# Four banks for the scores of two head pairs, and a new order of the weighted values

## The chip, the cores and the metric

The kernel runs on one core of one Trainium2 chip. The metric is the time of one execution on the device, in microseconds (us). The engines are named as the profile names them: PE is TensorE (PEld its weight loads, which overlap the matmuls), DVE is VectorE, ACT is ScalarE, POOL is GpSimd, and SP issues the transfers (DMAs). The execution that was profiled ran at a mean granted TensorE clock of 0.999 of full speed.

## What is computed

Windowed attention with eight global keys, for 4 batches, 8 heads, 768 positions and a head size of 64, and behind it a two-layer network with a gate. The inputs are float32.

```python
scores = scale * q @ k.T                       # per batch and head, 768 x 768
keep = is_global | is_local                    # keys 0..7, or the last 96 keys
scores = where(keep, scores - slope[h] * dist, -1e9)
a = exp(scores - max); a = a / (sum(a) + 1e-9)
x = (a @ v) as (3072, 512)                     # all heads side by side
h = x @ w_in                                   # 512 -> 2048
g = h * clip(h + 3, 0, 6) / 6
out = g @ w_out                                # 2048 -> 512
```

## The kernel before

The 3072 rows of x are cut into eight blocks of 384 rows (a block is one half of a batch). Per block the attention has four head pairs, and the network has 16 slices f of 128 hidden columns. A slice is worked in two layers: `first` (L166) makes 12 matmuls of 128x384 into one PSUM bank named hp; `gate` (L177) reads that bank on ACT (L183, tile g) and on DVE (L184); `high` and `rest` split g into gh (POOL, L190) and gl (DVE, L197); `second` (L200) makes 9 matmuls of 128x512 into the three banks named acc. There is one buffer for g, so a gate waits until gl of the slice before is made.

Eight PSUM banks exist: three acc, two hp (`ps_h`, taken in turn), and one each named sp, tp and xp, which the letters s, t and x of `bank` (L232) stand for.

The program has three stages. Attention of the first blocks comes first, then a mixed stage, and then the stage that the change touches, "layers" (L645 to L661): the network of block i, for i = 2 to 7, with the attention of block i+1 strewn in between. `twos` (L490) works two slices at a time: two first layers, then the two second layers of the slices before. It yields four times for each two slices, so units 0 and 1 of every four stand behind the first layers and units 2 and 3 behind the second layers. `attention` (L713) hangs the attention of block i+1 on these units; TURNS says at which unit a pair starts. Of one pair:

- `scale` (L861): POOL multiplies the queries, one instruction (L865), a turn ahead.
- `packed` (L867): PE makes the scores of the pair, 24 small matmuls with 64 rows and 32 columns of the array, one bank for each of the two heads. The trace keeps two records of each. I call such a visit to small matmuls an excursion.
- `weigh` (L900): DVE adds the distances and takes the least value (L908), six times per pair, and ACT makes the exponentials (L912), six per pair.
- `sum_up`, `normalize` (POOL, L932, six per pair), `spread` (DVE transposes into the tile `blocks`, L954, six per pair) and `send` (L956): SP issues four DMAs from `blocks` into the tile `weights`. The pool of `blocks` has one buffer, so the spread of the next pair waits until these DMAs have landed.

When all four pairs of a block are there, `weighted` (L688) multiplies weights and values in two excursions at units 25 and 26, four pairs at a time in four banks, one of them an hp bank. `put_x` (L155) reads each bank on ACT (xh) and on DVE (xl), and the result is x of the next block.

On PE, POOL and SP the program's order holds (`in_order`, L665). On DVE and ACT a scheduler sets the order, from estimates of its own.

## Time and profile before

| | |
|---|---|
| time, median of 3 runs | 647.18 us (646.72 to 648.17) |
| the profiled execution | 647.65 us, of which the span is 645.9 us |
| PE busy | 634.3 us (98%) |
| DVE busy | 354.9 us (55%) |
| ACT busy | 255.9 us (40%) |
| POOL busy | 167.4 us (26%) |
| DMA traffic | 59.78 MB, 93 GB/s on average |

A busy share is an average over the whole span. A busy PE is not the same as a PE that does useful columns: matmuls overlap in the record, so what an excursion costs is read from the starts of the matmuls around it. Times in rows count from the start of the span.

### The profile page before, as it was taken

How to read it: one execution, taken by the hardware profiler on the slowest of the kernel's cores; microseconds unless marked ns; L12 is line 12 of the kernel's file. 1: busy time of each engine (PE TensorE's matmuls, PEld its weight loads, DVE VectorE, ACT ScalarE, POOL GpSimd, SP SyncE). 2: the span in 40 equal slices, each digit the busy share in tenths (PEclk: the TensorE clock that was granted, in tenths of full speed). 3: DMA queues.
4: the chain of work that ended last, by engine and by line, in shares of the span. 5: the costliest groups of instructions: out<-in, count | busy, mean ns of one | idle time of the engine just before them, and what ended most of it. 6: DMA issues, size and time to landing. Idle time of an engine off the chain costs nothing.

```text
span 645.9 us, 14423 instructions
## 1 busy us (share of the span) xinstructions
PE 634.3 (98%) x5593; PEld 557.5 (86%) x5593; DVE 354.9 (55%) x1066; ACT 255.9 (40%) x706; POOL 167.4 (26%) x371
## 2 busy tenths in 40 slices
PE   9989999999999999999999999999999999999997
PEld 7768999888888888888888888888888888899985
DVE  5889999996645552455534564255623555222222
ACT  5897877775415321242223231143212522221111
POOL 4668000000422441124302332033311242012100
PEclk9999999999999999999999999999999999999999
DMA  7675554543334421242232241223312311110001
GB/s 280 173 227 178 161 159 135 159 135 126 96 73 144 100 79 31 71 123 70 60 98 75 63 102 48 67 79 86 92 31 69 106 33 31 33 50 1 1 1 54
DMA packets 34334, 59.78 MB, mean 93 GB/s; under 512 B 3280, under 2 KB 21200, under 8 KB 33488
## 3 DMA queue, kind: packets, MB, share of 16 engines
q1 hardware_dynamic: 33968, 58.50, 31.4%
q8 instruction: 46, 0.75, 0.5%
q14 instruction: 32, 0.26, 0.1%
q10 hardware_dynamic: 288, 0.26, 0.1%
HBM read 41.16 MB, written 6.29 MB: 73 GB/s over the span
## 4 chain that ended last, share of the span: by engine, by line
PE 89%; DVE 4%; ACT 3%; DMA 1%; POOL 1%; issue 1%; SPq 0%; POOLq 0%; ACTq 0%; DVEq 0%
PE hp L172 40%; PE acc L204 36%; PE sp L879 2%; DVE xl L159 2%; PE sp L204 2%; PE tp L204 1%; PE xp L204 1%; PE sp L706 1%; ACT n L912 1%; DMA wst<-w 1%; POOL n L932 1%; PE tp L706 1%; DMA load<-pairs 1%; PE xp L972 1%; PE sp L897 1%
## 5 line engine op out<-in xcount | busy, mean ns | idle before, releaser
L183 ACT ACTIVATE g<-hp,small 128x384 f32<-128x384 f32 x127 | 73.8, 581 | 261.3 <-PE hp L172 174.5
L172 PE MATMUL hp<-xh,w1h 128*128 128x384 f32 x512 | 174.2, 340 | 0.7 <-DVE xl L159 0.3
L172 PE MATMUL hp<-xh,w1l 128*128 128x384 f32 x512 | 172.4, 337 | 0.1
L172 PE MATMUL hp<-xl,w1h 128*128 128x384 f32 x512 | 171.7, 335 | 0.0
L190 POOL TENSOR_SCALAR gh<-g 128x384 fp32r<-128x384 f32 x104 | 53.5, 515 | 424.4 <-DVE g L184 397.6
L184 DVE SCALAR_TENSOR_TENSOR g<-g,hp 128x384 f32<-128x384 f32 x128 | 70.7, 552 | 122.0 <-ACT g L183 120.7
L204 PE MATMUL acc<-w2h,gh 128*128 128x512 f32 x336 | 133.2, 396 | 0.0
L204 PE MATMUL acc<-w2h,gl 128*128 128x512 f32 x336 | 131.9, 393 | 0.0
L204 PE MATMUL acc<-w2l,gh 128*128 128x512 f32 x336 | 131.7, 392 | 0.0
L197 DVE TENSOR_TENSOR gl<-g,gh 128x384 fp32r<-128x384 f32 x128 | 71.4, 558 | 66.4 <-POOL gh L190 59.0
L172 PEld LDWEIGHTS hp<-xh,w1h 128*128 128x128 f32 x512 | 96.1, 188 | 7.0 <-DVE xl L159 2.3
L912 ACT ACTIVATE n<-n,least 128x136 f32<-128x136 f32 (+2 forms) x192 | 79.9, 418 | 54.2 <-DVE least L908 53.4
L172 PEld LDWEIGHTS hp<-xl,w1h 128*128 128x128 f32 x512 | 96.1, 188 | 2.6
L172 PEld LDWEIGHTS hp<-xh,w1l 128*128 128x128 f32 x512 | 96.1, 188 | 0.9 <-DVE w1l L439 0.8
L932 POOL TENSOR_SCALAR n<-n,sums 128x136 f32<-128x136 f32 (+2 forms) x186 | 82.4, 460 | 39.7 <-DVE sums L923 23.8
L204 PEld LDWEIGHTS acc<-w2h,gh 128*128 128x128 f32 x336 | 63.1, 188 | 15.4 <-issue 3.8
L204 PEld LDWEIGHTS acc<-w2h,gl 128*128 128x128 f32 x336 | 63.0, 188 | 13.8 <-DVE gl L197 0.3
L204 PEld LDWEIGHTS acc<-w2l,gh 128*128 128x128 f32 x336 | 63.1, 188 | 11.3
L954 DVE STREAM_TRANSPOSE blocks<-n 128x256 f32<-128x256 f32 x138 | 51.2, 424 | 22.8 <-POOL n L932 21.4
L912 ACT ACTIVATION_READ_ACCUMULATOR n<-n,least 128x1 f32 x192 | 36.3, 189 | 0.0
L399 ACT ACTIVATE wz<-wst 128x512 f32<-128x512 f32 x32 | 21.6, 679 | 5.7 <-DVE w2l L439 3.9
L446 DVE CUSTOM_DVE_ANT_0 wz<-wz,we 128x1024 uint16<-128x1024 uint16 x32 | 22.2, 695 | 1.3 <-POOL we L404 0.9
(126 smaller groups left out, 728.6 us busy)
## 6 DMA issues: line engine op xcount, KB each, us to landing
wst<-w SPq DMA_DIRECT2D x32, 512.0 KB, 3.6
load<-pairs SPq DMA_DIRECT2D x31, 444.0 KB, 3.5
weights<-blocks SPq DMA_DIRECT2D x92, 120.0 KB, 2.4
values<-values SPq DMA_DIRECT2D x6, 1024.0 KB, 5.4
out<-o SPq DMA_DIRECT2D x23, 256.0 KB, 2.4
values<-pairs SPq DMA_DIRECT2D x9, 384.0 KB, 3.6
out<-o ACTq DMA_DIRECT2D x1, 256.0 KB, 3.0
load<-pairs SPq DMA_DIRECT2D x1, 252.0 KB
```

What stands on the lines that cost most here:

```text
L159: nc.vector.tensor_tensor(out=xl[:, pair, :], in0=ps, in1=xh[:, pair, :].bitcast(F32), op=ALU.subtract)
L172: self.nc.tensor.matmul(hp, lhsT=self.w1(w, f)[:, kt, :], rhs=a[:, kt, :], start=(n == 0), stop=(n == 3 * NKT - 1))
L183: nc.scalar.activation(out=g, in_=hp, func=AF.Relu, bias=self.three, scale=1.0)
L184: nc.vector.scalar_tensor_tensor(out=g, in0=g, scalar=6.0, in1=hp, op0=ALU.min, op1=ALU.mult)
L190: self.nc.gpsimd.tensor_scalar(out=gh, in0=g, scalar1=1.0, scalar2=0.0, op0=ALU.mult, op1=ALU.add)
L197: self.nc.vector.tensor_tensor(out=gl, in0=g, in1=gh.bitcast(F32), op=ALU.subtract)
L204: self.nc.tensor.matmul(acc[tt], lhsT=a[:, tk], rhs=self.w2(w, f), start=(f == 0 and j == 0), stop=(f == NF - 1 and j == 2))
L399: self.nc.scalar.activation(out=self.z[i].bitcast(F32), in_=words[:, :, 1].bitcast(F32), func=AF.Abs)
L446: tt(out=z, in0=z, in1=self.e.pop(i), op=ALU.add)
L912: nc.scalar.activation(out=e[:, j, lo:end], in_=e[:, j, lo:end], func=AF.Exp, bias=self.least[:, i:i + 1], scale=-1.0, accum_out=self.sums ...
L932: nc.gpsimd.tensor_scalar(out=e[:, j, lo:end], in0=e[:, j, lo:end], scalar1=over, scalar2=0.0, op0=ALU.mult, op1=ALU.add)
L954: nc.vector.transpose(out=self.blocks[:, :, t, 4 * s:4 * s + 4], in_=e[:, :, c:c + P].rearrange("p j (b q) -> p j b q", b=4))
```

## The change

Three things change, all for the stage "layers" (`weighted` is also called once at the end of the mixed stage, for three pairs).

The four pairs of a block no longer start at units 0, 5, 10 and 16, but two at unit 2 and two at unit 14. The first of the two takes an hp bank and the bank xp for its scores, the second takes sp and tp as before. DVE and ACT take the first pair head by head, so that the hp bank is read first. The second of the two pairs normalizes, spreads and sends two units later than the first. The pool `up` gets 6 buffers instead of 3. In `weighted`, pair 0, whose bank is hp, is now first in the order of the matmuls and not last.

```diff
-TURNS = (0, 5, 10, 16)
+TURNS = (2, 14)
...
-        self.up = self.pool("up", 3, side="right")
+        self.up = self.pool("up", 6, side="right")
...
-        for pair in pairs[::-1]:
+        for pair in pairs:
             bank = self.bank("xts"[pair.pr - 1]) if pair.pr else self.ps_h.tile([P, BANK], F32, name="hp")
...
-            at = units[TURNS[p]:]
-            at[0] += [me.packed] + [a.scale for a in (after,) if a] + [lambda me=me: self.load_next(me.n, False)]
+            at = units[TURNS[p // 2]:]
+            if p % 2 == 0:
+                at[0] += [lambda me=me: me.packed(True), after.scale, lambda me=me: self.load_next(me.n, False)]
+            else:
+                at[0] += [me.packed] + [a.scale for a in (after,) if a] + [lambda me=me: self.load_next(me.n, False)]
+                at = at[2:]
...
-    def packed(self):
+    def packed(self, first=False):
...
-        banks = [kk.bank(b)[:, 0:NT * PW].rearrange("p (t c) -> p t c", t=NT) for b in "st"]
+        banks = [kk.ps_h.tile([P, BANK], F32, name="hp"), kk.bank("x")] if first else [kk.bank("s"), kk.bank("t")]
+        banks = [bank[:, 0:NT * PW].rearrange("p (t c) -> p t c", t=NT) for bank in banks]
...
-        for t in range(NT):
-            self.weigh(t, [bank[:, t] for bank in banks], kk.up.tile([P, 2, PW], F32, name="n"), 0)
+        self.rows = [kk.up.tile([P, 2, PW], F32, name="n") for _ in range(NT)]
+        for heads in ((0,), (1,)) if first else ((0, 1),):
+            for t in range(NT):
+                self.weigh(t, [bank[:, t] for bank in banks], self.rows[t], 0, heads)
...
-    def weigh(self, t, sp, e, lo):
+    def weigh(self, t, sp, e, lo, heads=(0, 1)):
...
-        for j in range(2):
+        for j in heads:
```

What follows are three places of the built program, before and after.

On POOL, the attention of block 3, the first one in this stage. load_73 and load_74 are the queries of its pairs 1 and 2 (the L865 or L869 row is `scale`), gh belongs to the network, n are the normalizations. Before:

```order
L190 TENSOR_SCALAR gh<-g 128x384 x5
L865 TENSOR_SCALAR load_73<-load_73,over 128x384
L932 TENSOR_SCALAR n<-n,sums 128x136 x4
L190 TENSOR_SCALAR gh<-g 128x384 x2
L932 TENSOR_SCALAR n<-n,sums 128x136 x2
L865 TENSOR_SCALAR load_74<-load_74,over 128x384
```

After:

```order
L869 TENSOR_SCALAR load_73<-load_73,over 128x384
L869 TENSOR_SCALAR load_74<-load_74,over 128x384
L190 TENSOR_SCALAR gh<-g 128x384 x2
L939 TENSOR_SCALAR n<-n,sums 128x136 x10
L190 TENSOR_SCALAR gh<-g 128x384 x2
L939 TENSOR_SCALAR n<-n,sums 128x136 x2
```

Pair 1 is scaled at the same place as before, behind the gh of the first two slices, but its scores now follow at once on PE; the normalizations of two pairs stand together.

On ACT, the same block up to `put_x`. n,sums is the exponential of `weigh`, g the gate, xh the first half of `put_x`. Before:

```order
L912 ACTIVATE n,sums<-n,least 128x136 x6
L183 ACTIVATE g<-hp,small 128x384 x4
L912 ACTIVATE n,sums<-n,least 128x136 x6
L183 ACTIVATE g<-hp,small 128x384 x4
L158 CAST xh<-sp 128x384
L158 CAST xh<-tp 128x384
L158 CAST xh<-xp 128x384
L158 CAST xh<-hp 128x384
```

After:

```order
L920 ACTIVATE n,sums<-n,least 128x136 x12
L183 ACTIVATE g<-hp,small 128x384 x6
L158 CAST xh<-hp 128x384
L158 CAST xh<-xp 128x384
L158 CAST xh<-tp 128x384
L158 CAST xh<-sp 128x384
```

Twelve exponentials stand in one piece ahead of the next gate, and the hp bank of `weighted` is read first and not last.

On DVE, from the last sums of the block's pairs to `put_x` (blocks is the spread, L954 before and L961 after). Before:

```order
L923 RECIPROCAL sums<-sums 128x6
L954 STREAM_TRANSPOSE blocks<-n 128x2x128 x4
L184 SCALAR_TENSOR_TENSOR g<-g,hp 128x384
L197 TENSOR_TENSOR gl<-g,gh 128x384
L184 SCALAR_TENSOR_TENSOR g<-g,hp 128x384
L197 TENSOR_TENSOR gl<-g,gh 128x384
L954 STREAM_TRANSPOSE blocks<-n 128x2x128 x2
```

After:

```order
L197 TENSOR_TENSOR gl<-g,gh 128x384
L961 STREAM_TRANSPOSE blocks<-n 128x2x128 x6
L184 SCALAR_TENSOR_TENSOR g<-g,hp 128x384
L197 TENSOR_TENSOR gl<-g,gh 128x384
L184 SCALAR_TENSOR_TENSOR g<-g,hp 128x384
L961 STREAM_TRANSPOSE blocks<-n 128x2x128 x2
L197 TENSOR_TENSOR gl<-g,gh 128x384
L961 STREAM_TRANSPOSE blocks<-n 128x2x128 x4
```

The six spreads of pair 2 now stand in the same stretch as those of pair 3, ahead of them; on SP the eight DMAs of two sends follow each other with no load between.

## Rows read from the trace of the kernel before

**Rows 1.** The page, chain that ended last: shares of the span by engine.

```profile
PE 89%; DVE 4%; ACT 3%; DMA 1%; POOL 1%; issue 1%; SPq 0%; POOLq 0%; ACTq 0%; DVEq 0%
```

**Rows 2.** Timeline around one excursion: start, duration, engine, line, operation, [idle before].

```profile
205.45 0.34 PE L172 MATMUL hp<-xh,w1l 128*128 128x384 f32 x1
205.72 0.10 PEld L879 LDWEIGHTS sp<-load 64*32 64x32 f32 x1 [0.25 <-issue]
...
206.41 0.28 PE L879 MATMUL tp<-load 64*32 64x136 f32 x1
...
206.61 0.50 PE L204 MATMUL acc<-w2h,gh 128*128 128x512 f32 x1
...
206.95 0.40 PE L204 MATMUL acc<-w2l,gh 128*128 128x512 f32 x1
```

**Rows 3.** The chain in order of time: start, us, what (x24 two first layers).

```profile
295.99 4.36 PE hp L172 x24
300.35 4.12 PE acc L204 x18
304.47 4.19 PE hp L172 x24
...
326.35 2.09 PE acc L204 x9
```

**Rows 4.** Timeline behind the weighted values of block 3, PE and DVE.

```profile
260.94 0.55 DVE L159 TENSOR_TENSOR xl<-hp,xh 128x384 fp32r<-128x384 f32 x1
...
261.06 0.34 PE L172 MATMUL hp<-xh,w1l 128*128 128x384 f32 x1
261.54 0.44 PE L172 MATMUL hp<-xh,w1h 128*128 128x384 f32 x1
261.82 0.34 PE L172 MATMUL hp<-xl,w1h 128*128 128x384 f32 x1
```

**Rows 5.** Waits of PE's weight loads: us in total, times, longest.

```profile
PEld hp L172 <- DVE xl L159: 2.3, 5, 0.5
```

**Rows 6.** Timeline at the first excursion of block 3, PE and POOL.

```profile
200.46 0.30 PE L879 MATMUL sp<-load 64*32 64x136 f32 x1
...
202.39 0.52 POOL L190 TENSOR_SCALAR gh<-g 128x384 fp32r<-128x384 f32 x1 [2.04 <-DVE g L184]
202.88 0.60 POOL L865 TENSOR_SCALAR load<-load,over 128x384 f32<-128x384 f32 x1
```

**Rows 7.** Timeline of an excursion of the mixed stage that met an idle DVE.

```profile
158.16 0.73 PEld L879 LDWEIGHTS acc<-load 64*32 64x32 f32 x48 [0.37 <-POOL gh L190]
...
159.23 0.30 DVE L908 CUSTOM_DVE_ANT_0 n<-acc,dl 128x136 f32<-128x136 f32 x1 [0.61 <-PE acc L879]
...
159.57 0.41 ACT L912 ACTIVATE n<-n,least 128x136 f32<-128x136 f32 x1 [0.70 <-DVE least L908]
```

**Rows 8.** Timeline of one pair from exponentials to send (ACT, DVE, SP).

```profile
297.00 0.41 ACT L912 ACTIVATE n<-n,least 128x136 f32<-128x136 f32 x1 [4.94 <-DVE least L908]
...
299.38 0.57 ACT L183 ACTIVATE g<-hp,small 128x384 f32<-128x384 f32 x1
...
304.90 2.20 DVE L954 STREAM_TRANSPOSE blocks<-n 128x256 f32<-128x256 f32 x6 [0.56 <-POOL n L932]
...
307.13 2.54 SPq L960 DMA_DIRECT2D weights<-blocks  x4
```

**Rows 9.** Timeline of two sends close together in the mixed stage (SP and DVE).

```profile
167.59 2.69 SPq L960 DMA_DIRECT2D weights<-blocks  x4
...
172.19 0.77 DVE L954 STREAM_TRANSPOSE blocks<-n 128x256 f32<-128x256 f32 x2 [1.44 <-DMA weights<-blocks]
...
174.76 2.54 SPq L960 DMA_DIRECT2D weights<-blocks  x4
```

**Rows 10.** Last send of block 3, and the first matmul of its weighted values.

```profile
246.53 2.56 SPq L960 DMA_DIRECT2D weights<-blocks  x4
...
252.57 0.54 PE L706 MATMUL sp<-weights,values 32*64 32x384 f32 x2
```

## The prediction

> **What bounds the kernel now.** I read the shares of the chain that ended last first: PE holds 89% of it [rows 1], so time is gained where PE does less or waits less, and lost where PE comes to wait for something. Busy time cannot tell the two apart, so the second view is the timeline around one excursion [rows 2]. The reader is to look at starts. The last large matmul starts at 205.45, the second large one behind the excursion at 206.95: 1.50 us. Without an excursion the same two steps would take one first-layer pitch (4.18 / 24 = 0.17, from the 4.19 of two first layers) and one second-layer pitch (4.12 / 18 = 0.23) [rows 3]: 0.40. So an excursion costs 1.10. The starts of its 48 small records spread over 205.72 to 206.41, which is 0.69 [rows 2]; the other 0.41 goes into the turn from large to small matmuls and back. The third view is the waits of PE's weight loads: in this stage the large one is that on `put_x`, five times [rows 5], seen in the timeline behind the weighted values [rows 4]. Last I read the way of one pair through ACT, POOL, DVE and SP [rows 8, 9], because that way has to end before `weighted` starts.

> **Merged excursions.** Five blocks have four excursions each now, and two each afterwards. The 48 records of a second pair add 0.69 if they go on at the same pitch, and the turn of 0.41 is paid once and not twice. Ten turns fewer: 10 x 0.41 = **4.1 us less** [rows 2]. This is PE's own time, so nothing hides it. The bounds are 0.38 and 0.45 each, since the starts are given to 0.01 and the pitch varies by as much: 3.8 to 4.5.

> **The first layer's bank read first.** Before, the hp bank of `weighted` is the last that DVE reads (260.94, 0.55 long), and slice 15's first layer, whose bank it is, starts at 261.54, 0.48 behind the matmul before it instead of 0.17; the next matmul follows at 0.28, again 0.11 late [rows 4]. Together 0.42, five times: **2.1 us less**; without the 0.11 it is 1.6. Afterwards DVE reads this bank as the first of four, three readings of 0.55 or a little less earlier, so it is free over 1 us sooner, while 0.3 is needed. What is late next there is PE itself.

> **Pair 1 of block 3 waits for POOL.** `scale` of a pair is issued right in front of its own scores for pairs 1 and 3. In most places that is harmless: the second layers of two slices (4.12 [rows 3]) lie between the first layers and unit 2, and POOL is through by then. In block 3 there is nothing to finish yet at unit 2, so PE goes straight from the first layers into pair 0. POOL's order has the two gh first, then the scaling, which ends at 202.88 + 0.60 = 203.48 [rows 6]; the change moves none of these. Pair 0 starts at 200.46 and pair 1 could follow 0.69 later, at 201.15. PE waits 2.3, and I add 0.1 for the signal, an estimate: **2.4 us more, once** (2.3 to 2.6). Behind the waiting matmul stands all of PE's queue.

> **The weights of pair 3 come later.** This is the largest unknown. Pairs 2 and 3 start at unit 14, and `weighted` stands at unit 25. Before, the last send of block 3 starts at 246.53 and its four DMAs have landed some 4.5 later, about 251.0, while `weighted` starts at 252.57 [rows 9, 10]: 1.5 to spare. Now count from T, the start of the merged excursion. DVE's first score comes at T + 1.07 and ACT's first exponential at T + 1.41 [rows 7]. Twelve exponentials in one piece, ahead of the next gate, take twice the 2.38 that six take [rows 8]: T + 6.17. From that gate to the send of the first pair (two gates, six normalizations, six spreads) the same order stands in one place of the trace and takes 299.38 to 307.13, 7.75 [rows 8]: send of pair 2 at T + 13.9. `blocks` has one buffer, so DVE may not spread pair 3 before these four DMAs have landed. One such wait is in the trace: 167.59 to 172.19, 4.60 [rows 9]. Its four issues took 2.69; with the 2.54 of the other sends it would be 4.45. So T + 18.4 to 18.5. From there two spreads, another operation and four spreads, the order that the change has here, took 172.19 to 174.76, 2.57 [rows 9]: second send at about T + 21.0, landed at T + 25.4 to 25.7. PE meanwhile: 0.89 to the first large matmul [rows 2], 0.69 for the second pair, and then six large pieces, of which the first is 4.36 and the last 2.09, with 4.12, 4.19, 4.12 and 4.18 between [rows 3]: it stands in front of `weighted` at about T + 24.65. The wait is 0.75 to 1.05 by these rows; I take 0.95, near the upper end, since every hop adds a little that I left out. Five blocks: **4.8 us more**. For the range I allow 0.6 to 1.3 each, 3.0 to 6.5. Whoever waits here is PE with all that stands behind it; its first three pairs' weights are there and help nothing, since the fourth follows in the same queue.

> **The rest costs nothing.** Head 0's bank is wanted by the second first layer behind the excursion, at 0.89 + 0.69 and half of 4.36 behind T, T + 3.8 [rows 2, 3]. DVE reads its three scores from T + 1.07 on [rows 7], faster than ACT takes three exponentials (1.2 [rows 8]): it is free by T + 2.3. The gates come 2.4 later, behind six more exponentials [rows 8]; the banks that they free are wanted only after two first and two second layers, some 8 us on [rows 3]. If this cover failed, PE would wait at the third first layer. The buffers of `up` take away a wait of DVE that no row shows PE waiting for. `load_next` moves with the scores on SP; `scale` wants the loads only at the excursion after.

> **The sum.** -4.1 - 2.1 + 2.4 + 4.8 = **+1.0 us**. The profiled execution took 647.65, 0.47 over the median; the same step on the median of 647.18 gives **648.2**. Terms at their ends: -4.5 - 2.1 + 2.3 + 3.0 = -1.3 and -3.8 - 1.6 + 2.6 + 6.5 = +3.7, so 645.9 to 650.9.

> **Rivals.** *The weights land in time* (0.10). If POOL or DVE get through the chain a microsecond faster, the five waits vanish and the sum is -4.1 - 2.1 + 2.4 = -3.8: 643.4. For it: the spare time is only 1 us short, and the 7.75 holds pieces that depend on when gates fall. Against it: each piece is one that the trace shows in that order.

> *The merged excursion saves nothing* (0.08); this one ends slower and also means that the change doesn't do what it says. The second pair needs its own start-up: new banks and new row and column places, another 0.41. Then ten times 0.41 come back, but the five in front of `weighted` are taken out of PE's wait there: +1.0 + 4.1 - 2.1 = +3.0, 650.2. It decides if the starts of the second 48 records leave a gap of more than 0.3 behind the first. Against it: within the 48 records of one pair the array takes new weights all the time, without a gap.

> *The scores are not read out in time* (0.04). Twelve scores lie in four banks at once, read by one DVE. If DVE came 3 us late, the second first layer would wait about 1.5 us in each of ten excursions, which also lets the weights land in time: +1.0 + 15 - 4.8 = +11, 658. It would take over from a delay of 1.5 (T + 2.3 against T + 3.8). Against it: no spread and no long operation stands ahead of the scores on DVE in the new order. [...]

> The remaining 0.04 is for what I don't see.

> **How the numbers follow.** The forecast has 0.74. Its own spread, 645.9 to 650.9, holds nearly all of that, and the second rival too; 645.0 to 651.0 holds about 0.8. About 0.2% (1.3 us) is what a measurement of this kernel can tell from no change: 645.9 and 648.5 are the marks. Of the forecast's 0.74 about 0.45 lie between, 0.27 above, 0.02 below. With the first rival, and some of the unseen, faster is 0.13; with the second and third, slower is 0.42; same 0.45.

> **What would show it.** Merged excursions whose small records start over some 1.4 us with no gap inside; no wait for xl at slice 15 of blocks 3 to 7's attention; one wait of 2.4 in PE near 201 to 203.6, released by POOL; and five waits of about 0.95 at `weighted`, released by the DMAs of `weights`, with DVE's first spread of pair 3 waiting for the DMAs of pair 2 ahead of each. It would be wrong if the last waits are absent or twice as long, if `put_x` still reads the hp bank last, or if the granted clock falls in one of the new gaps.

## The result and the profile after

The changed kernel took 650.67 us (median of five runs, 648.55 to 651.5), the kernel before 647.18: a ratio of 1.005, 95% interval 1.0028 to 1.0071. It is slower by 3.5 us, half a per cent. That lies in the predicted range (645.0 to 651.0), 2.5 us above the predicted 648.2, and in the class "slower" by the prediction's own marks (above 648.5), which had 0.42 against 0.45 for "same". The execution that was profiled took 648.55, close to the forecast; the other four took 650.1 to 651.5. The profiled one ran at a mean granted clock of 1.000, the four at 0.996 to 0.997. So there are two things to explain: the sum of the edits, which the trace shows, and some 2.4 us more in the other four runs (their mean is 650.9), which it does not show.

The page of the changed kernel: busy time of each engine, the granted clock in 40 slices of the span, and the chain that ended last (PE's share is 87% now, against [rows 1]).

```profile
span 646.7 us, 14369 instructions
...
PE 631.9 (98%) x5593; PEld 558.8 (86%) x5593; DVE 352.4 (55%) x1066; ACT 254.7 (39%) x706; POOL 169.3 (26%) x371
...
PEclk9999999999999999999999999999999999999999
...
PE 87%; DVE 4%; ACT 4%; POOL 2%; DMA 2%; issue 1%; SPq 0%; POOLq 0%; DVEq 0%; ACTq 0%
```

A merged excursion in the timeline of the changed kernel (start, duration, engine, line, operation), the answer to [rows 2]: from the last large start, 228.64, to the second large one behind it, 230.85.

```profile
228.64 0.39 PE L204 MATMUL acc<-w2h,gl 128*128 128x512 f32 x1
228.96 0.30 PE L884 MATMUL hp<-load 64*32 64x136 f32 x1
...
230.57 0.44 PE L172 MATMUL hp<-xh,w1h 128*128 128x384 f32 x1
230.85 0.34 PE L172 MATMUL hp<-xl,w1h 128*128 128x384 f32 x1
```

That is 2.21 us, and nine of the ten excursions read so. The 96 small starts spread over 1.41 with no gap above 0.10. Two single excursions cost 2 x (1.50 - 0.40) = 2.20 beyond the large matmuls, the merged one 2.21 - 0.40 = 1.81: 0.39 saved, ten times 3.9.

The waits of the changed kernel (us in total, times, longest), first PE's and its weight loads', then DVE's:

```profile
PE sp L884 <- POOL load L869: 2.1, 1, 2.1
```

```profile
PEld sp L884 <- POOL load L869: 2.4, 1, 2.4
PEld hp L172 <- DVE least L916: 1.9, 9, 0.2
```

```profile
DVE blocks L961 <- DMA weights<-blocks: 20.3, 11, 2.9
```

The row of [rows 5], the first layer's wait for `xl`, has no successor. In its place stand one wait for POOL's scaling, and eleven waits of DVE for the transfers out of `blocks` (in the kernel before there was one, of 1.4). The latter come out at the weighted values. The timeline of those of block 5 shows it:

```profile
403.70 0.54 PE L706 MATMUL hp<-weights,values 32*64 32x384 f32 x2
...
404.95 0.54 PE L706 MATMUL sp<-weights,values 32*64 32x384 f32 x2 [0.37 <-issue]
...
405.30 0.78 PE L706 MATMUL sp<-weights,values 32*64 32x384 f32 x9
```

Pairs 0 to 2 start at 403.70, pair 3 (bank sp) 1.25 later. The large matmuls around it, first before and then after (the last one ahead, the second one behind):

```profile
403.28 0.40 PE L204 MATMUL acc<-w2h,gl 128*128 128x512 f32 x1
...
406.29 0.39 PE L204 MATMUL acc<-w2l,gh 128*128 128x512 f32 x1
```

```profile
403.37 0.40 PE L204 MATMUL acc<-w2h,gl 128*128 128x512 f32 x1
...
407.49 0.40 PE L204 MATMUL acc<-w2l,gh 128*128 128x512 f32 x1
```

That is 3.01 and 4.12. Measured in this way, the first halves of the weighted values (the first of their two excursions) of blocks 3 to 7 took 3.65, 3.27, 4.12, 3.26 and 4.41, against 3.01, 2.67, 3.01, 2.68 and 3.02 before: 4.3 us more together.

So the trace gives -3.9 - 2.1 + 2.4 + 4.3 = +0.7, and the span went from 645.9 to 646.7, by 0.8. That these two agree so well is in part chance, as the two executions did not run alike ahead of the stage that was changed. Here are one matmul of the mixed stage and the last matmul of all, before and after:

```profile
177.19 0.40 PE L204 MATMUL tp<-w2h,gl 128*128 128x512 f32 x1
...
640.75 0.40 PE L204 MATMUL acc<-w2h,gl 128*128 128x512 f32 x1
```

```profile
176.64 0.40 PE L204 MATMUL tp<-w2h,gl 128*128 128x512 f32 x1
...
641.25 0.39 PE L204 MATMUL acc<-w2h,gl 128*128 128x512 f32 x1
```

The profiled execution of the changed kernel was 0.55 earlier at the first of these (most of it, 0.47, was there at 27 us already), and from it to the last matmul it took 464.61 against 463.56, 1.05 more. The rows above name 0.7 of that; the other 0.35 is in no single wait. Behind the last matmul it took 0.3 more. The further 2.4 us of the other runs are the question of the experiments.

### The profile page after: what moved, and what is told of

The parts are those of the page before. It is cut to its first block, busy times and chain, and to the rows that moved or that the text cites. A ratio compares the mean times of both kernels' runs of the same rounds, so it can differ in the third digit from the quotient of the medians.

```text
span 646.7 us, 14369 instructions
## 1 busy us (share of the span) xinstructions
PE 631.9 (98%) x5593; PEld 558.8 (86%) x5593; DVE 352.4 (55%) x1066; ACT 254.7 (39%) x706; POOL 169.3 (26%) x371
## 4 chain that ended last, share of the span: by engine, by line
PE 87%; DVE 4%; ACT 4%; POOL 2%; DMA 2%; issue 1%; SPq 0%; POOLq 0%; DVEq 0%; ACTq 0%
PE hp L172 40%; PE acc L204 35%; ACT n L920 2%; PE sp L204 2%; PE tp L204 1%; PE xp L204 1%; PE hp L706 1%; PE sp L706 1%; PE hp L884 1%; POOL n L939 1%; DMA weights<-blocks 1%; DMA iv<-bounds 1%; DVE n L916 1%; PE sp L884 1%; PE tp L706 1%
## 5 line engine op out<-in xcount | busy, mean ns | idle before, releaser
L172 PE MATMUL hp<-xh,w1h 128*128 128x384 f32 x512 | 174.1, 340 | 0.0
L172 PE MATMUL hp<-xh,w1l 128*128 128x384 f32 x512 | 172.3, 337 | 0.1
L172 PE MATMUL hp<-xl,w1h 128*128 128x384 f32 x512 | 171.7, 335 | 0.0
L204 PE MATMUL acc<-w2h,gh 128*128 128x512 f32 x336 | 131.6, 392 | 0.0
L172 PEld LDWEIGHTS hp<-xh,w1h 128*128 128x128 f32 x512 | 96.1, 188 | 5.4 <-DVE least L916 1.9
L172 PEld LDWEIGHTS hp<-xl,w1h 128*128 128x128 f32 x512 | 96.1, 188 | 2.5
L172 PEld LDWEIGHTS hp<-xh,w1l 128*128 128x128 f32 x512 | 96.1, 188 | 0.9 <-DVE w1l L439 0.8
L939 POOL TENSOR_SCALAR n<-n,sums 128x136 f32<-128x136 f32 (+2 forms) x186 | 80.3, 452 | 17.1 <-DVE sums L930 12.3
L961 DVE STREAM_TRANSPOSE blocks<-n 128x256 f32<-128x256 f32 x138 | 50.6, 420 | 27.8 <-DMA weights<-blocks 20.3
```

The lines of the kernel that those rows point to most:

```text
L172: self.nc.tensor.matmul(hp, lhsT=self.w1(w, f)[:, kt, :], rhs=a[:, kt, :], start=(n == 0), stop=(n == 3 * NKT - 1))
L204: self.nc.tensor.matmul(acc[tt], lhsT=a[:, tk], rhs=self.w2(w, f), start=(f == 0 and j == 0), stop=(f == NF - 1 and j == 2))
L939: nc.gpsimd.tensor_scalar(out=e[:, j, lo:end], in0=e[:, j, lo:end], scalar1=over, scalar2=0.0, op0=ALU.mult, op1=ALU.add)
L961: nc.vector.transpose(out=self.blocks[:, :, t, 4 * s:4 * s + 4], in_=e[:, :, c:c + P].rearrange("p j (b q) -> p j b q", b=4))
```

## The experiments

Each kernel is compared with runs of the kernel before on the same chip (medians 647.31, 647.30 and 647.44 in the three groups), "against before" below. The clocks are means over the span, one for each run. The lower level behind the last matmul (0.68 over the last 1.9 us of the kernel before's profile, 0.95 over the last 2.7 us of the changed kernel's) counts in them too, so the profiled runs without a fall of the clock in the work show 0.998 to 1.000, those with one fall 0.995 to 0.997, and `e7_second_earlier`, with two, 0.993. The kernel before showed 0.998 or more in 40 of its 41 runs there.

### One part alone

`e5_values_first` is the kernel before with the second part of the change only.

```diff
-        for pair in pairs[::-1]:
+        for pair in pairs:
```

> The kernel before, with one part of the change alone: of the weighted values, the pair whose bank is the first layer's is computed and read out first (the pairs run from 0 to 3, not from 3 to 0). The prediction has 0.42 us for each of the five waits of the first layer for its left operand, so 2.1 us: a median of 645.1, and the row of that wait gone. The rival, by which the same wait only goes to the pair that is now last, which the scores behind it need: 647.2, the kernel before's time, with a wait of about 0.4 us at the start of the next bank.

Measured: 645.20 (644.94 to 645.89), 2.1 less than before, ratio 0.997, interval 0.9957 to 0.9982, clocks 0.998 to 1.000. The wait for `xl` at L172 is gone from its rows, and no gap stands in the next bank's place. The term of 2.1 holds, and this part alone makes the kernel faster.

`e6_turns_only` is the changed kernel with that line put back, so the merged excursions alone.

> The changed kernel without its second part: the weighted values are computed and read out in the order of before, pair 3 first. By the prediction's term of 0.42 us for each of five blocks the wait of the first layer for its left operand comes back: 2.1 us over the changed kernel, a median of 652.8, and the row of that wait stands again with 5 times and some 0.4 to 0.5 us. The rival: in the merged order pair 3's weights come last anyway, so starting with them makes the wait for the weights longer too, by up to one chunk's three other pairs (0.1 us), and the time is 653.3. If the two parts overlap, so that the wait for the weights already covers the other, the time stays at 650.7.

Measured: 653.90 (652.73 to 655.16), 6.6 more than before and some 3.2 more than the changed kernel. The wait for `xl` is back (PEld hp L172: 2.3, 5, 0.5), worth 2.1. That leaves about 1.1. The weighted values grew too: their first halves took 20.5 in all, 6.1 more than before, against 4.3 in the changed kernel's profile. The timeline of block 5 shows how:

```profile
406.47 0.40 PE L204 MATMUL acc<-w2h,gl 128*128 128x512 f32 x1
408.47 0.54 PE L706 MATMUL sp<-weights,values 32*64 32x384 f32 x2 [1.59 <-DMA weights<-blocks]
408.70 0.54 PE L706 MATMUL tp<-weights,values 32*64 32x384 f32 x2
```

With pair 3 first nothing runs until its weights land, 2.0 behind the last large start. With pair 3 last the other three pairs' first matmuls stand in that time, as the rows of block 5 above show. I had priced this at 0.1 at most. By these two profiles it is 0.36 each, by the 1.1 left in the medians 0.2. Its size is not settled, since the first halves vary from run to run by as much (below). The two parts of the change are thus not independent: the new order of reading also softens the wait that the merging makes.

### Where the clock falls

`e1_scale_early`: the scaling of pair 1 of block 3 is issued ahead of the block loop.

```diff
+        Pair(self, 3 * NPAIR + 1, None, False).scale()
         for i in range(2, len(self.blocks)):
...
-                at[0] += [lambda me=me: me.packed(True), after.scale, lambda me=me: self.load_next(me.n, False)]
+                at[0] += [lambda me=me: me.packed(True)] + [after.scale] * (n != 3 * NPAIR) + [lambda me=me: self.load_next(me.n, False)]
```

> The changed kernel, with one step put earlier: the scaling on POOL of pair 1 of block 3, for which TensorE waited 2.4 us between the two halves of that block's first excursion, is issued ahead of the block loop. The same values are computed. Both theories: the gap of 2.37 us in front of the second half of that excursion goes, and the excursion takes 2.2 us instead of 4.5. Theory G, by which the four runs of the changed kernel at a mean granted clock of 0.996 to 0.997 lost their further 2 to 3 us because TensorE's clock fell at this gap: every run comes back to a granted clock of 0.999 or 1.000, and the median falls by 2.3 and by 2.1 more, from 650.7 to about 646.3, 0.9 under the kernel before. Theory W, by which the clock falls at one of the five waits for the weights of pair 3 (0.6 to 1.4 us each): the clocks stay at 0.996 to 0.997 in most runs, and the median falls by 2.3 alone, to 648.4.

Measured: 648.31 (647.44 to 650.08), 1.0 more than before. The wait is gone: the excursion takes 2.35 instead of 4.5. Of eleven runs seven show 0.998 to 1.000 (647.4 to 648.5) and four 0.994 to 0.996 (649.4 to 650.1). Neither theory is right alone. With the gap of block 3 gone seven of eleven runs keep the clock, where three of ten of the changed kernel did, which points to the gap without proving it; four lose it all the same. The profiled run is one of these, and its windows (time, PE busy, granted clock, DMA) show where:

```profile
554.00:555.50 1.50, 0.00 (x0) 1.00 0.59 113
555.50:557.00 1.50, 1.50 (x80) 1.00 0.00 0
557.00:557.50 0.50, 0.50 (x41) 0.57 0.00 0
557.50:560.00 2.50, 2.50 (x34) 0.50 0.03 7
560.00:560.50 0.50, 0.50 (x2) 0.52 0.00 0
560.50:561.00 0.50, 0.50 (x4) 1.00 0.00 0
```

PE came to a gap of 2.16, from start to start, for the weights of pair 3 of block 7 (in the changed kernel's profile the costliest such wait was 1.4). After it had gone on, the clock fell to 0.50 for 3.4 us; half of that, 1.7, is the most it can have cost, an estimate from these two numbers. In this run the first halves of the weighted values took 21.1 in all, 6.7 more than before and the most of any, so part of what the earlier scaling saved was lost there.

`e4_scale_late` goes the other way:

```diff
+        for _ in range(4 if self.n == 3 * NPAIR + 1 else 0):
+            nc.gpsimd.tensor_scalar(out=q, in0=q, scalar1=1.0, scalar2=0.0, op0=ALU.mult, op1=ALU.add)
```

> The changed kernel, with four more multiplications by one on POOL ahead of the scaling of pair 1 of block 3 (0.76 us each by the two that stand there, 1.53 together, so 3.1 us); the values stay the same. Both theories: the gap in that block's first excursion grows from 2.4 to about 5.4 us. Theory G: the clock falls at this gap in every run, also the profiled one, whose windows behind the gap show a granted clock under 1.00; the median is 650.7 plus 3.1, 653.8, or some 2 us more where the longer gap costs more. Theory W: the windows behind the gap stay at 1.00, and where the clock falls it falls behind a wait of the weighted values; the median is 653.8.

Measured: 654.08 (653.63 to 654.40), 6.8 more than before; all four runs at 0.993 to 0.997. The gap is 5.1. Windows of the profiled run:

```profile
201.00:205.00 4.00, 0.00 (x0) 1.00 0.37 114
205.00:206.00 1.00, 0.40 (x20) 0.88 0.00 0
206.00:209.00 3.00, 3.00 (x48) 0.50 0.23 39
209.00:210.00 1.00, 1.00 (x7) 0.92 0.82 327
```

Again 3.4 us at the lower level, directly behind the gap. Counted from the first start behind the gap, the following large matmuls start 1.6 later than the same ones of the changed kernel's profiled run, which kept its clock: that is the price of this fall. Does the shorter gap of the changed kernel do the same? In `e6_turns_only`, where it is 2.38, the profiled run shows it:

```profile
201.00:202.00 1.00, 0.00 (x0) 1.00 0.25 28
202.00:203.00 1.00, 0.13 (x8) 0.86 0.81 259
203.00:206.00 3.00, 3.00 (x53) 0.50 0.29 83
206.00:206.50 0.50, 0.50 (x4) 0.86 0.69 206
```

Here the same count gives 1.4.

The changed kernel's own profiled run has the same gap, 2.37, and keeps the clock:

```profile
201.00:202.00 1.00, 0.00 (x0) 1.00 0.13 18
202.00:203.00 1.00, 0.03 (x5) 1.00 0.77 217
203.00:206.00 3.00, 3.00 (x60) 1.00 0.48 159
```

So the same idle time lowers the clock in some executions and not in others.

### Is it the idle time, or the wait?

`e9_filled` and `e12_late_filled` leave the wait and take away TensorE's idleness: matmuls of a constant into banks that the scores overwrite. In the first these are 144 small ones in the changed kernel; in the second, 22 of full size in the kernel with the late scaling.

```diff
+        for t in range(3 * NT if self.n == 3 * NPAIR + 1 else 0):
+            for g in range(GROUPS):
+                for j in range(2):
+                    nc.tensor.matmul(banks[j][g * GQ:(g + 1) * GQ, t % NT, 0:P], lhsT=kk.ident[j * D:(j + 1) * D, 0:GQ],
+                                     rhs=kk.ident[j * D:(j + 1) * D], start=True, stop=True, tile_position=(j * D, g * GQ))
```

```diff
+        for i in range(22 if self.n == 3 * NPAIR + 1 else 0):
+            nc.tensor.matmul(banks[i % 2][:, 0, 0:P], lhsT=kk.ident, rhs=kk.ident, start=True, stop=True)
```

> The changed kernel, with TensorE kept at work in the gap of block 3: ahead of the second half of that excursion stand 144 small matmuls of a constant into the same two banks, which the scores overwrite; at the 14.7 ns from start to start of the scores they take 2.1 us of the 2.37. The wait for POOL stays as long, and the result is the same. Theory G (TensorE's idle time is what the clock falls for): the excursion takes 4.5 us as before, but the clock no longer falls behind it; only the waits for the weights can still lower it, as in 4 of 11 runs of the kernel with the early scaling, so the median is 648.5 to 649.0 and most runs show 0.998 or more. The rival (the fall hangs on the wait for POOL or on what else runs at that place): the clocks stay at 0.996 to 0.997 in most runs and the median at 650.7. The small matmuls run late themselves and push the scores back: 0.3 to 1 us on top of either.

Measured: 648.79 (648.20 to 650.06), 1.5 more than before, nine runs of nine at 0.998 to 1.000. The small matmuls left a hole of 1.1 in their own middle, of which 0.85 is put down to issue, and so ran late: the starts of the excursion's scores spread over 4.6 instead of 3.7. Even so the median is 1.9 under the changed kernel's (2.0 when each is taken against before on its own chip, 1.3 against `after_again` in the same way). The clock of the profiled run is at 1.00 from the gap to 645 us, when the last matmul has ended.

> The kernel with the late scaling (four more multiplications by one on POOL, a gap of 5.1 us in block 3, 654.1 us with clocks of 0.993 to 0.997 in all its runs), with 22 matmuls of a constant of 128 by 128 into the two banks ahead of the second half of the excursion, which the scores overwrite; at an estimated 0.21 us each they fill 4.7 of the 5.1 us. The wait for POOL stays, and the result is the same. If the clock falls for TensorE's idle time, it stays at 1.00 behind the excursion, and the median is the changed kernel's undisturbed 648.5 plus 2.8 for the longer wait, 651.3, with up to 1 us more in runs in which it falls behind a wait for the weights. By the rival (the fall hangs on the wait itself or on the other work there) the clock falls here as it did without the filling: 654.1.

Measured: 649.64 (649.05 to 650.13), 2.2 more than before, six runs of six at 0.999 or 1.000. Its windows:

```profile
201.00:206.00 5.00, 5.00 (x56) 1.00 0.31 92
206.00:207.00 1.00, 1.00 (x51) 1.00 0.00 0
207.00:211.00 4.00, 4.00 (x35) 1.00 0.40 120
```

The 22 matmuls, estimated at 0.21 each, start 0.22 apart behind the first (201.44 to 205.91).

`after_again` is the changed kernel on the chip of `e12_late_filled`.

> The changed kernel once more, on the chip of the other kernels of this job. If the further 2 us of its median come from falls of the clock behind its gaps, a run that shows under 0.998 has in its profile a stretch of about 3.5 us at 0.50 right behind the gap of block 3 or behind a wait of the weighted values, and the others none; the median is 650.7, and the runs at 0.999 or 1.000 lie at 648.5. The rival: the clock's fall belongs to the chip on which the change was first timed, and all runs here lie at 648.5.

Measured: 650.19 (648.93 to 651.54), ratio 1.0047, interval 1.0033 to 1.0061: two runs at 0.999 (648.93 and 649.70), three at 0.996 (650.19 to 651.54). So it is no matter of one chip. The profiled run was one of the two, so the fall itself was not caught in the changed kernel's own profile.

The kernel with the longer wait is 0.5 us faster than the changed one. With the same wait of 5.1 the clock was down in four runs of four where TensorE was idle (654.1, 6.8 over before), in none of six where it was busy (2.2 over before). By these runs the fall goes with the idle time and not with the wait. Of these 4.6 us 1.6 are the clock at the lower level, by the count above. The rest, by the two profiles, is that the weights came earlier in the filled one: its first halves of the weighted values took 17.4 in all, against 19.5 in `after_again` and 20.2 in the unfilled one. That difference was not expected, and its cause stays open.

### Why the weights of pair 3 come late

`e2_two_blocks` gives the spread weights a second buffer. The space is taken from the output rows, which fall from three buffers to one.

```diff
-        self.bp = self.pool("bp", 1, side="right")
+        self.bp = self.pool("bp", 2, side="right")
...
-        self.op = self.pool("op", 3, side="right")
+        self.op = self.pool("op", 1, side="right")
```

> The changed kernel, with two buffers instead of one for the spread weights from which a pair's transfers are sent; the space comes from the output rows, which get one buffer instead of three. The same values are computed. If the weights of pair 3 come late because the one buffer makes pair 3's spreading on DVE wait for pair 2's transfers (11 waits of DVE, 20.3 us in all in the profile of the changed kernel), the five waits at the start of the weighted values go: excursions of 3.0 and 2.7 us, 4.3 us less, so 644.3 in a run whose profile shows a clock of 1.000 and 646.4 in one whose clock falls in block 3. If they come late because the excursion of pairs 2 and 3 stands later, whatever the buffers, the five waits stay and so does the time, 648.5 to 650.7. The single output buffer can add up to 2 us at the ends of the blocks.

Measured: 652.97 (651.82 to 653.53), clocks 0.990 to 0.993. The time says nothing, because the single output buffer costs more than I allowed: PE waits for the output rows in the mixed stage (1.9, at 159 us) and in block 3's first excursion (1.2), the clock falls behind both places, and everything from there on starts some 6 to 10 us later than in the changed kernel. The mechanism can be read all the same. The first halves of the weighted values take 3.01, 2.68, 3.01, 2.67 and 3.01: all five waits are gone, and the row "DVE blocks <- DMA" with them. DVE now waits only for POOL's normalization; PE has new waits:

```profile
DVE blocks L961 <- POOL n L939: 13.2, 23, 0.9
```

```profile
PE acc L884 <- ACT o L60: 1.9, 1, 1.9
PE xp L884 <- ACT o L60: 1.2, 1, 1.2
```

The later start can't have made this: from the start of the second merged excursion to the weighted values PE takes 24.68 in each of the five blocks, and 24.70 in the changed kernel. With PE's own pace the same and the buffer doubled, the waits go. It was the one buffer, as the prediction had it.

### A version without the waits

`e7_second_earlier` moves the second excursion from unit 14 to unit 10.

```diff
-TURNS = (2, 14)
+TURNS = (2, 10)
```

> The changed kernel, with the second merged excursion of each block four units of work earlier (at unit 10 instead of 14), so that pairs 2 and 3 send their weights some 11 to 13 us earlier. The same values are computed. Both theories: the five waits at the start of the weighted values go (4.3 us in the profile of the changed kernel), the gap of 2.4 us in block 3 stays. Theory G (the clock falls at the gap in block 3): clocks of 0.996 to 0.997 in most runs, and a median 4.3 under the changed kernel, 646.4. Theory W (it falls at the waits for the weights): every run at 0.999 or 1.000, and 4.3 and 2.1 less, 644.3. If the wait was not for the transfers of pair 3 but for something that moving the excursion leaves in place, the waits stay and so does the time, 650.7.

Measured: 651.40 (650.40 to 651.68), 4.1 more than before. The waits for the weights are gone (3.01 and 2.67), as both theories had it, but neither time held: two new waits stand in the second excursions of blocks 3 and 7, 1.60 and 2.57, both for POOL:

```profile
PE sp L884 <- POOL load L869: 5.7, 3, 2.3
```

In the profiled run the clock also fell to 0.50 twice, behind block 3's gap of 2.36 and behind the one of 2.57.

`e10_ahead_earlier` also moves the scaling two units forward, in both excursions.

```diff
+                units[TURNS[p // 2] - 2].append(after.scale)
-                at[0] += [lambda me=me: me.packed(True), after.scale, lambda me=me: self.load_next(me.n, False)]
+                at[0] += [lambda me=me: me.packed(True), lambda me=me: self.load_next(me.n, False)]
```

> The changed kernel with two moves: the scaling on POOL of the second pair of every merged excursion is issued two units of work ahead of the excursion, and the second excursion of a block stands at unit 10 instead of 14. The same values are computed. If what the change lost was the waits (2.4 us once for the scaling, 4.3 us for the weights of pair 3) and the falls of TensorE's clock behind them, nothing is left of either: excursions of 2.2 us with no gap over 0.1, weighted values of 3.0 and 2.7 us, a granted clock of 0.998 or more in every run, and a median of 647.2 less 3.8 and 2.1, so 641.3. The rival: the clock falls for another reason than these gaps, and most runs stay at 0.993 to 0.997, some 2 to 4 us more: 643.5 to 645.5. A second rival: the scaling, two units earlier, stands on POOL ahead of a part that the first layers wait for, and gaps of about 0.5 us appear there, ten times: 646.

Measured: 649.19 (648.82 to 651.09), 1.9 more than before; three runs at 0.999, three at 0.994 to 0.997. The three gaps stayed, at 2.38, 2.65 and 2.55. POOL's timeline at the second one shows why:

```profile
221.69 0.52 POOL L190 TENSOR_SCALAR gh<-g 128x384 fp32r<-128x384 f32 x1 [5.00 <-PE xp L885]
222.19 1.14 POOL L940 TENSOR_SCALAR n<-n,sums 128x136 f32<-128x136 f32 x2
223.31 1.15 POOL L870 TENSOR_SCALAR load<-load,over 128x384 f32<-128x384 f32 x2
```

Unit 8 and unit 10 stand behind the same gate parts (gh) on POOL. Two units earlier in the list was no place earlier in its queue, and the scaling still came behind a gh and two normalizations. `e11_no_waits`, with the second excursion at unit 10 as well, puts it at unit 7, ahead of those gh, and for pair 1 of block 3 ahead of the block loop.

```diff
+        Pair(self, 3 * NPAIR + 1, None, False).scale()
...
+                if p:
+                    units[TURNS[1] - 3].append(after.scale)
-                at[0] += [lambda me=me: me.packed(True), after.scale, lambda me=me: self.load_next(me.n, False)]
+                at[0] += [lambda me=me: me.packed(True)] + [after.scale] * (p == 0 and n != 3 * NPAIR) + [lambda me=me: self.load_next(me.n, False)]
```

> The changed kernel without its waits: the scaling of pair 1 of block 3 is issued ahead of the block loop, as in the kernel with the early scaling; the second merged excursion of a block stands at unit 10 instead of 14; and the scaling of pair 3 is issued at unit 7, which POOL reaches one pair of slices earlier (two units earlier, at unit 8, stand behind the same parts on POOL as unit 10, and the three waits for the scaling stayed). The same values are computed. Both the wait for POOL and the waits for the weights should be gone, and with them the falls of the clock: excursions of 2.2 us without a gap over 0.1, weighted values of 3.0 and 2.7 us, clocks of 0.998 or more, and a median of 647.2 less 3.8 and 2.1, so 641.3. By the rival a fall of the clock that hangs on the merged excursions themselves stays (0.993 to 0.997): 643.5 to 645.

Measured: 643.56 (643.22 to 647.39), ratio 0.9936, interval 0.9922 to 0.9949: 3.9 less than before and faster than both kernels. Five of six runs show 0.998 to 0.999. The sixth, at 0.997, is the profiled one; it met a wait of 2.6 for ACT near 57 us, ahead of everything that the change touches, with a fall of the clock behind it (second-layer matmuls start 0.43 apart from 58.18 on, 0.23 at 57.35), and this is its 647.39. From block 3 on its trace has neither the wait for POOL nor those for the weights: ten excursions of 2.21 to 2.35, weighted values of 3.01 and 2.67. What is missing to the expected 641.3 stands in the first layers, as three new gaps of 0.7, 0.2 and 0.85 us beyond the usual pitch. The first, at 226.89, is put down to DVE's reading of the scores (L919), so the prediction's third rival does come here, once and small. The largest, on PE, and DVE's rows to it:

```profile
467.24 0.34 PE L172 MATMUL hp<-xh,w1l 128*128 128x384 f32 x1
468.26 0.45 PE L172 MATMUL hp<-xh,w1h 128*128 128x384 f32 x1 [0.68 <-DVE g L184]
```

```profile
466.67 1.10 DVE L964 STREAM_TRANSPOSE blocks<-n 128x256 f32<-128x256 f32 x3 [2.77 <-DMA weights<-blocks]
467.69 0.52 DVE L184 SCALAR_TENSOR_TENSOR g<-g,hp 128x384 f32<-128x384 f32 x1
```

DVE waits 2.77 for the one buffer, a gate stands behind that on DVE, and a first layer waits for the gate. -3.9 - 2.1 + 0.1 + 1.8 = -4.1, against -3.9 measured.

## Why the prediction was right, and where it was not

- **Merged excursions** (-4.1; measured -3.9). The mechanism holds: one turn saved each time, no gap between the two pairs' records. It is 0.39 and not 0.41, near the lower bound. The rival by which it saves nothing is out.
- **The first layer's bank read first** (-2.1). Measured as -2.1 alone, and from the rows in the changed kernel. It does a second thing that the prediction did not see, as it runs the other pairs' matmuls inside the wait for pair 3.
- **Pair 1 of block 3 waits for POOL** (+2.4). The gap is 2.37, the row 2.4. No row stood behind the 0.1 that was added for the signal; the gap bears the sum out.
- **The weights of pair 3 come later** (+4.8; measured +4.3 in the first profile, 5.1 in `after_again`). The waits are 0.5 to 1.4 and not alike; the prediction counted one block's way and took it five times. Its T + 24.65 for PE was 24.7 in every block, so what varies is when the weights land. In the kernels with the same work there the sum went from 3.0 (`e12_late_filled`) to 6.7 (`e1_scale_early`), so that 4.8 came so close is in part luck. Its cause, the one buffer, is shown by `e2_two_blocks`. The rival of weights that land in time is out.
- **The rest costs nothing.** True for the scores: the weight loads' waits on DVE there are 0.2 each (1.9 in nine), and they cost PE no time, since behind the excursions no two matmuls of a first layer start more than 0.28 apart, as before. The rival by which the four banks are not read out in time (658) did not come in the changed kernel.
- **The sum** of +1.0 stands against +0.7 in the rows and +1.05 on PE from the mixed stage on, and 648.2 against 648.55 for the execution that kept its clock. The step that failed is the price of a wait: both were priced at their length alone. Behind gaps of 2.16 to 5.1 the profiles of `e1_scale_early`, `e4_scale_late` and `e6_turns_only` show TensorE's clock at 0.50 for 3.4 us, 1.4 to 1.6 us lost by the counts above, and by the mean clocks the changed kernel had such a fall in most runs: it was at 0.996 to 0.997 in seven of its ten, with means 2.4 and 1.6 us above its other runs. The prediction named this among what would make it wrong ("if the granted clock falls in one of the new gaps"), but gave it neither a price nor a chance. The trace that it had could not show one: its gaps, up to 1.70 from start to start (43.22 to 44.92), had left the clock at 1.00. With the term, the median is 648.2 + 1.5 = 649.7, and "slower" would have been the likeliest class. The measured 650.67 and 650.19 are 0.5 to 1.0 above that; the weights (0.8 between the two profiles) and the start of an execution (0.5) vary by as much, but which of them it was is not shown. That the median still lies in the range owes as much to luck: its upper end was made for longer waits for the weights and has nothing for the clock, and four of the changed kernel's ten runs lie above 651.0.

That the fall in the changed kernel's runs is the one seen in `e6_turns_only` and `e1_scale_early` is inferred: the same gaps, a mean clock that fits one fall, and the fall's absence when the gap is filled. It was not caught in a trace of the changed kernel itself. What decides in which executions a gap of 2.4 lowers the clock stays open: `e10_ahead_earlier` has three such gaps in its profiled run and stays at 0.999.

## What to carry to other kernels

Price a new wait of TensorE at its length and, with a chance of its own, at a fall of the clock behind it as well (1.4 to 1.6 us here where TensorE was busy throughout; `e10_ahead_earlier`'s two runs at 0.997 were only 0.5 above those at 0.999); where the wait can't go, harmless matmuls into a bank that is about to be overwritten kept the clock (0.998 to 1.000 in nine runs of nine of `e9_filled`, 0.999 or 1.000 in six of six of `e12_late_filled`). When work is packed closer together, look at what has one buffer or one queue behind it: here the saving of 0.39 per merged excursion was paid for by one `blocks` buffer and one scaling on POOL. An instruction moved forward here only where it moved in its own engine's queue: in `e10_ahead_earlier` two units earlier in the list were no place earlier on POOL, and the gaps stayed at 2.38 to 2.65.
